# Pooled attention and two feed-forward networks on one core: the probability transpose as one vector instruction and twenty copies inside SBUF

## The chip, the core and the metric

The kernel runs on one core of a Trainium2 chip. The core has a matrix engine (TensorE, PE in the profile, with its weight loads shown as PEld), a vector engine (VectorE, DVE), a scalar engine (ScalarE, ACT), a general engine (GpSimd, POOL) and an engine that here only issues transfers (SyncE, SP). SBUF is the on-chip memory, with 128 partitions; PSUM is the memory that TensorE writes. The metric is the device time of one execution in microseconds (us). The kernel before took 1600.52 us (median of 3 runs, 1599.71 to 1601.85).

## The reference

```python
# q, k, v: (8 batches, 8 heads, 576 tokens, 64), float32
k_p = k.reshape(B, H, 72, 8, D).mean(axis=3)         # pooled over 8 tokens
v_p = v.reshape(B, H, 72, 8, D).mean(axis=3)
scores = (1 / sqrt(D)) * q @ k_p.T                   # 576 x 72 per head
attn = exp(scores - max); attn = attn / (sum(attn) + 1e-9)
x = (attn @ v_p) as 4608 tokens x 512
a, b = x @ w1, x @ w2                                # 512 -> 1024
x2 = (a * b) @ w3 @ w_out                            # 1024 -> 1024 -> 512
h = x2 @ w_in2                                       # 512 -> 2048
out = (h * sigmoid(1.702 * h)) @ w_out2              # 2048 -> 512
```

The weights arrive as float64 and are converted on the chip.

## The kernel before, in words

Every large product is made of three float32r passes: an operand is held as a rounded "hi" part and the exact rest "lo", and hi*hi, hi*lo and lo*hi are added in PSUM (`mm3`, L95 to L97). A TensorE instruction multiplies 128 rows by 512 columns.

The work has three stretches. First w3 @ w_out is formed, while the weights are converted (`Conv`) and the first batch's attention runs beside it. Then comes the first network: nine blocks of 512 tokens, and in each block eight steps f. A step makes a and b for 128 of the 1024 features (24 matmuls into the PSUM tiles wk0 and wk1, one tile for a and one for b), forms u = a * b (ACT copies a out of PSUM on L517, DVE multiplies on L518, ACT and POOL split it on L90 and L91), and two steps later adds u's contribution to x2 (12 matmuls into the four tiles acc). At the end of a block x2 is copied out (L486, L488) and stored to DRAM by SP (L489). Last comes the second network, of the same form.

Attention is done in 32 groups, a pair of heads of one batch each. A group is cut into pieces, and the function `tick` emits one piece at a time between the matmuls: two ticks in each step f, four ticks to a group. The pieces, for group n:

- `g0`: k and q are turned on DVE (L229 into the tile kT, L230 into qT), k is summed over the pool (L232, tile ks), and SP issues the loads of the next group's k and q (8 loads, L203).
- `g1`: scores on TensorE into wk2 and wk3 (L246, ten matmuls), maximum and difference on DVE (L251, L253) into the tile s_t, tokens on partitions.
- `g2`: the exponential on ACT (L261). `g_va` beside it averages v on POOL (L291 to L299) and loads the next v (L223, L224).
- `g3`: sum, reciprocal and normalisation on DVE (L267 to L270). Then the probabilities must be turned so that keys lie on partitions: p0 holds 128 keys, p1 the remaining 16, padded to 32. For the first four groups TensorE does that in `g4` (L318 to L329). For the 28 others DVE does it with 32x32 block transposes: 20 instructions (L281), one for each of 5 key blocks and 4 token blocks, which write the turned blocks to their final place. This is the part that changes.
- `g4`: p0 and p1 are split into ph and pt (ACT L335, L337, L338; POOL L336, L339).
- `g6`: probabilities times values on TensorE (L347 to L350, four matmuls for each of two halves, into wk2 and wk3), and the result is split into the block's input x (ACT L357, DVE L358).

A block of the first network needs, of all four head pairs, the tokens that it covers, so block b waits for group 4b+3. The tiles kT, s_t, p0, p1, ph, pt and qT have one buffer each: who writes one waits for the last reader of its previous content. wk2 and wk3 serve both the scores and the products with the values.

The order in which the instructions stand on each engine isn't the order of the code: a list scheduler reorders them when the program is built, by the code's order as priority and by its own estimate of when each instruction becomes ready. On the chip each engine then works through its own list strictly in order. SP too: a transfer that waits holds up those behind it. Transfers on SP signal eight semaphores in turn, so the ninth waits until the first has landed.

Of the kernel before, what the change touches and what calls it, by code (L numbers as in the profile page):

```python
# [7 lines left out]
F32 = mybir.dt.float32  # L8
# [9 lines left out]
P = 128  # L18
# [4 lines left out]
def pooled_attention_moe_moe2(  # L23
# [10 lines left out]
    w_out2: bass.AP,  # L34
    out: bass.AP,
):
    """Matrix products in three float32r passes: every operand x is held as
    hi = x rounded to 12 significant bits and lo = x - hi (exact), and
    x*y = hi*hi + hi*lo + lo*hi.  The scores take plain float32 products.
    Features lie on partitions and tokens along the free axis up to the last  # L40
    product, which puts tokens back on partitions."""
    nc = tc.nc
    B, H, S, D = q.shape
    NT, DM = out.shape
# [4 lines left out]
    w1, w2, w3, w_out, w_in2, w_out2 = (w.bitcast(U32) for w in (w1, w2, w3, w_out, w_in2, w_out2))  # L49
# [8 lines left out]
    TT = (S + P - 1) // P  # L58
    KW = 2 * SK
    PW = 160  # L60
# [9 lines left out]
    free = [(slot_p, i) for i in range(NSLOT)]  # L70
    held = {}
# [10 lines left out]
    def give(*ts):  # L82
        for t in ts:
            free.append(held.pop(id(t))[1:])
# [6 lines left out]
        lo_eng.tensor_tensor(out=dst[:, 1], in0=src, in1=f32(dst[:, 0]), op=ALU.subtract)  # L91

    def mm3(o, a, a_sl, b, b_sl, first, last):
        """o += a[:, a_sl].T @ b[:, b_sl] of two hi/lo pairs."""
        nc.tensor.matmul(o, a[:, 0, a_sl], b[:, 0, b_sl], start=first, stop=False)  # L95
        nc.tensor.matmul(o, a[:, 0, a_sl], b[:, 1, b_sl], start=False, stop=False)  # L96
        nc.tensor.matmul(o, a[:, 1, a_sl], b[:, 0, b_sl], start=False, stop=last)  # L97
# [7 lines left out]
    def sl(i, n=P):  # L105
        return slice(i * n, (i + 1) * n)

    class Conv:
        """float64 words (low, high) to float32, rounded to nearest, then to hi/lo.
        |w| < 2^-119 stays below that bound, but not exact."""  # L110

        def __init__(self):
            self.todo, self.staged, self.line = [], [], [None, None]
# [19 lines left out]
                self.staged.append((t, turn, done))  # L133

        def step(self):
            """float32 of the next chunk, transpose of the last, hi/lo of the one before."""
            new = None
            if self.staged:
                t, turn, done = self.staged.pop(0)
                lo_w, hi_w = t[:, :, 0], t[:, :, 1]  # L140
                w = cv_p[0].tile([P, T], F32, name="cv", tag="cv", bufs=4)
                wu = w.bitcast(U32)
                nc.scalar.activation(w, hi_w.bitcast(F32), AF.Copy, scale=2.0 ** -112)  # L143
                nc.scalar.activation(lo_w.bitcast(I32), lo_w, AF.Copy, scale=2.0 ** -29)
                nc.vector.tensor_scalar(  # L145
                    out=wu, in0=wu, scalar1=4, scalar2=1,
                    op0=ALU.logical_shift_left, op1=ALU.logical_shift_right)
                nc.vector.scalar_tensor_tensor(  # L148
                    out=wu, in0=hi_w, scalar=0x80000000, in1=wu,
                    op0=ALU.bitwise_and, op1=ALU.bitwise_or)  # L150
                nc.gpsimd.tensor_tensor(  # L151
                    out=w.bitcast(I32), in0=w.bitcast(I32), in1=lo_w.bitcast(I32), op=ALU.add)
                give(t)
                new = [w, turn, done]
            mid, old = self.line
            if mid and mid[1]:
                mid[0] = mid[1](mid[0])
            key = old[2](old[0]) if old else None
            self.line = [new, mid]
            self.load()  # L160
            return key
# [7 lines left out]
    with tc.tile_pool(name="pa", bufs=1) as pa:  # L169
        cv_p[0] = pa  # L170

# [1 line left out]
        mask = pa.tile([P, 2, D], F32, name="mask")  # L173
        nc.gpsimd.memset(mask, 1.0 / POOL)
        nc.gpsimd.affine_select(
            out=mask[:, 0], in_=mask[:, 0], compare_op=ALU.is_gt, fill=0.0,
            base=SK, pattern=[[0, D]], channel_multiplier=-1)
        nc.gpsimd.affine_select(
            out=mask[:, 1], in_=mask[:, 1], compare_op=ALU.is_ge, fill=0.0,
# [5 lines left out]
        s_t = pa.tile([P, TT, PW], F32, name="s_t")  # L185
# [6 lines left out]
            out=ident, in_=ident, compare_op=ALU.is_equal, fill=0.0,  # L192
# [2 lines left out]
        vt = pa.tile([96, 2 * D], F32R, name="vt")  # L195
        nc.gpsimd.memset(f32(vt), 0.0)

# [1 line left out]
        g_q, g_k, g_v, g_s = {}, {}, {}, {}  # L199

        def load_blocks(dst, src, b, hp):
# [61 lines left out]
        def g3(n):  # L263
            r = g_s.pop(n)
            pv = s_t[:, :, :KW].rearrange("p t (a s) -> p t a s", s=SK)
            rv = r.rearrange("p (t a) -> p t a", a=2)
            nc.vector.tensor_reduce(out=rv, in_=pv, op=ALU.add, axis=AX.X)  # L267
            nc.vector.tensor_scalar_add(r, r, 1e-9)
            nc.vector.reciprocal(out=r, in_=r)
            nc.vector.tensor_tensor(  # L270
                out=pv, in0=pv, in1=rv.unsqueeze(3).to_broadcast([P, TT, 2, SK]), op=ALU.mult)
            p0 = pa.tile([P, TT, P], F32, name="p0", tag="p0")
            p1 = pa.tile([32, TT, P], F32, name="p1", tag="p1")
            g_s[n] = (p0, p1)
            if n < NPE:
                return
            for r in range(5):
                for c in range(4):
                    nt = TT if 32 * (c + 1) <= S - (TT - 1) * P else TT - 1
                    dst = p0[32 * r:32 * r + 32] if r < 4 else p1[:32]  # L280
                    nc.vector.transpose(  # L281
                        out=dst[:, :nt, 32 * c:32 * c + 32],
                        in_=s_t[32 * c:32 * c + 32, :nt, 32 * r:32 * r + 32])

        def g_va(n):
            # values, averaged over the pool, in blocks of two heads
            vr, tr = g_v.pop(n), vtr
            a = pa.tile([P, 4 * D], F32, name="va", tag="va")
            at = pa.tile([32, 4 * D], F32, name="vat", tag="vat")
            for d, s in ((a, vr), (at, tr)):  # L290
                nc.gpsimd.tensor_tensor(out=d, in0=s[:, :4 * D], in1=s[:, 4 * D:], op=ALU.add)  # L291
                nc.gpsimd.tensor_tensor(
                    out=d[:, :2 * D], in0=d[:, :2 * D], in1=d[:, 2 * D:], op=ALU.add)
                nc.gpsimd.tensor_tensor(out=d[:, :D], in0=d[:, :D], in1=d[:, D:2 * D], op=ALU.add)
            vf = pa.tile([P, 2, D], F32, name="vf", tag="vf")
            nc.gpsimd.tensor_tensor(
                out=vf, in0=a[:, :D].unsqueeze(1).to_broadcast([P, 2, D]), in1=mask, op=ALU.mult)
            vtf = pa.tile([32, D], F32, name="vtf", tag="vtf")
            nc.gpsimd.tensor_scalar_mul(vtf, at[:, :D], 1.0 / POOL)  # L299
            g_v[n] = (vf.rearrange("p a d -> p (a d)"), vtf)  # L300
            v_load(n + 1)
# [93 lines left out]

        wo_s, wp_s, w1_s, w2_s, b_s1, b_s2 = {}, {}, {}, {}, {}, {}

# [1 line left out]
        NIT = DF1 // P  # L399
        w3_s = {}  # L400

# [13 lines left out]
            return done  # L415

        def w3_mm(key):
            """The products that the chunk that came last makes possible."""
            if isinstance(key, int):
                jts, its = [key], [it for it, jh in seen if jh == key // 4]  # L420
                seen_o.append(key)
            else:
                its, jts = [key[0]], [j for j in seen_o if j // 4 == key[1]]
                seen.append(key)
            for it in its:
                for j in jts:
                    n = n_mm[it] = n_mm.get(it, 0) + 1
                    mm3(acc[it % 4], w3_s[it, j // 4], sl(j % 4), wo_s[j], slice(0, T),
                        n == 1, n == NIT)
                    n4 = n_mm[it, j // 4] = n_mm.get((it, j // 4), 0) + 1  # L430
                    if n4 == 4:
                        give(w3_s.pop((it, j // 4)))
                        seen.remove((it, j // 4))
                    if n == NIT:
                        w = wp_s[it] = take()
                        split(w, acc[it % 4], nc.vector)

        n_mm, seen, seen_o = {}, [], []
        for half in range(2):
            for jh in range(2):  # L440
                for i in range(4):
# [4 lines left out]
                    it = half * 4 + i  # L446
# [20 lines left out]
        while tick_n[0] < 20:  # L467
            tick()

# [1 line left out]
        u_s = {}  # L471
        pend = []

# [28 lines left out]
        for blk in range(NB):  # L502
            x = [x_slot(blk, c) for c in range(KM)]
            for f in range(NF1):
# [11 lines left out]
                a = pa.tile([P, T], F32, name="a", tag="a", bufs=2)  # L516
                nc.scalar.copy(a, pa_)  # L517
                nc.vector.tensor_tensor(out=a, in0=pb_, in1=a, op=ALU.mult)  # L518
                u = u_s[blk, f] = take()
# [27 lines left out]
            conv.staged = st  # L547
        conv.todo = rest

# [1 line left out]
    with tc.tile_pool(name="pb", bufs=1, reuse_waits="tile") as pb_p:  # L551
        for i in range(5):
            free.append((pb_p, NSLOT + i))
# [21 lines left out]
        for blk in range(NB):  # L575
            x = x2n[blk]
            for f in range(NF2):
# [5 lines left out]
                a = pb_p.tile([P, T], F32, name="sg", tag="sg", bufs=3)  # L583
                nc.scalar.activation(a, ps, AF.Sigmoid, scale=1.702)  # L584
                nc.vector.tensor_tensor(out=a, in0=ps, in1=a, op=ALU.mult)  # L585
                g = g_sl[blk, f] = take()
# [45 lines left out]
```

## Time and profile before

| | |
|---|---|
| median of 3 timed runs | 1600.52 us (1599.71 to 1601.85) |
| profiled execution, first to last instruction (span) | 1599.4 us; the page gives no other time for it |
| PE busy | 1536.5 us, 96% |
| DVE busy | 756.8 us, 47% |
| ACT busy | 587.2 us, 37% |
| POOL busy | 714.2 us, 45% |
| granted TensorE clock, mean over the span | 0.982 of full speed |
| transfers on SP's queue | 195392 packets, 94.40 MB, 22.4% of 16 DMA engines' span |

A busy share is an average over the whole span. The first network's stretch runs from about 140 to 800 us; attention of the 28 groups whose transpose changes is over by about 655 us. In the profile a row "idle before <- X" names what ended the wait. Matmuls overlap, so a matmul's own duration (0.39 us) is longer than the distance to the next one.

### The profile page before, as it was taken

The numbers are of one execution on the slowest core, as the hardware profiler recorded it, in microseconds if no ns is written. First come the engines' busy times: TensorE is split into PE (matmuls) and PEld (weight loads), VectorE is DVE, ScalarE is ACT, GpSimd is POOL, SyncE is SP. The second block draws the span as 40 slices with busy tenths as digits, with TensorE's granted clock in tenths as the row PEclk, the third lists the DMA queues.
The fourth block names the chain that finished last, engine by engine and source line by source line (L and its number), as shares of the span: only waits on it lengthen the run. The fifth ranks groups of instructions, "written<-read, shape, count | busy, mean of one in ns | idle before, by whom it ended". The sixth has DMA issues, their size and how long they took to land.

```text
span 1599.4 us, 19097 instructions
## 1 busy us (share of the span) xinstructions
PE 1536.5 (96%) x6920; PEld 1267.0 (79%) x6920; DVE 756.8 (47%) x1458; ACT 587.2 (37%) x1130; POOL 714.2 (45%) x748
## 2 busy tenths in 40 slices
PE   5867999999999999999998999999999999999998
PEld 3645888888888888888786888888888888888887
DVE  8999987878787877214585111111111111111111
ACT  6874443433343334225554222222222222223221
POOL 6789654455555544225777232323222232323221
PEclk9977999999999999999999999999999999999999
DMA  9973232323232310024430000000010000000000
GB/s 277 244 156 58 52 72 50 78 49 72 52 72 45 75 46 34 27 80 158 146 104 27 27 27 27 20 32 20 9 40 14 33 20 33 21 27 14 27 0 27
DMA packets 195488, 95.62 MB, mean 60 GB/s; under 512 B 155457, under 2 KB 171841, under 8 KB 195393
## 3 DMA queue, kind: packets, MB, share of 16 engines
q1 hardware_dynamic: 195392, 94.40, 22.4%
q8 instruction: 54, 0.88, 0.2%
q14 instruction: 42, 0.34, 0.1%
HBM read 75.50 MB, written 18.87 MB: 59 GB/s over the span
## 4 chain that ended last, share of the span: by engine, by line
PE 82%; DVE 8%; issue 3%; DMA 2%; ACT 2%; POOL 2%; SPq 1%; DVEq 0%; POOLq 0%; ACTq 0%
PE wk L95 15%; PE wk L96 15%; PE wk L97 15%; PE acc L97 11%; PE acc L96 11%; PE acc L95 11%; DVE cv L148 2%; PE wk L246 2%; DVE cv L145 2%; DVE s L91 2%; DMA s<-in_moe_w_out_dram 1%; DVE p L281 1%; DMA s<-in_moe_w_dram 1%; POOL s L91 1%; ACT s L90 1%
## 5 line engine op out<-in xcount | busy, mean ns | idle before, releaser
L95 PE MATMUL wk<-s,s 128*128 128x512 f32 x1152 | 453.5, 395 | 7.6 <-DVE a L518 4.3
L96 PE MATMUL wk<-s,s 128*128 128x512 f32 x1152 | 451.4, 392 | 2.0 <-DVE s L358 2.0
L97 PE MATMUL wk<-s,s 128*128 128x512 f32 x1152 | 450.8, 392 | 1.4 <-DVE s L91 1.4
L91 POOL TENSOR_TENSOR s<-sg,s 128x512 fp32r<-128x512 f32 x144 | 188.6, 1310 | 508.8 <-ACT s L90 508.8
L585 DVE TENSOR_TENSOR sg<-wk,sg 128x512 f32<-128x512 f32 x144 | 99.6, 692 | 619.5 <-ACT sg L584 619.5
L97 PE MATMUL acc<-s,s 128*128 128x512 f32 x928 | 363.7, 394 | 9.5 <-DVE s L91 5.1
L95 PE MATMUL acc<-s,s 128*128 128x512 f32 x928 | 364.7, 395 | 4.3 <-ACT s L90 4.3
L96 PE MATMUL acc<-s,s 128*128 128x512 f32 x928 | 364.4, 393 | 1.6 <-DVE s L91 1.1
L95 PEld LDWEIGHTS wk<-s,s 128*128 128x128 f32 x1152 | 217.7, 189 | 54.5 <-DVE a L518 5.6
L97 PEld LDWEIGHTS wk<-s,s 128*128 128x128 f32 x1152 | 217.9, 189 | 47.5 <-DVE s L91 1.8
L96 PEld LDWEIGHTS wk<-s,s 128*128 128x128 f32 x1152 | 217.8, 189 | 46.9 <-DVE s L358 2.4
L584 ACT ACTIVATE sg<-wk 128x512 f32<-128x512 f32 x144 | 86.1, 598 | 410.9 <-PE wk L97 410.8
L97 PEld LDWEIGHTS acc<-s,s 128*128 128x128 f32 x928 | 175.6, 189 | 48.6 <-DVE s L91 8.2
L95 PEld LDWEIGHTS acc<-s,s 128*128 128x128 f32 x928 | 175.4, 189 | 41.5 <-ACT s L90 7.2
L96 PEld LDWEIGHTS acc<-s,s 128*128 128x128 f32 x928 | 175.8, 189 | 38.1 <-POOL s L91 1.8
L91 POOL TENSOR_TENSOR s<-a,s 128x512 fp32r<-128x512 f32 x72 | 94.1, 1307 | 215.8 <-ACT s L90 174.9
L281 DVE STREAM_TRANSPOSE p<-s_t 32x160 f32<-32x160 f32 (+1 forms) x560 | 178.4, 319 | 10.8
L151 POOL TENSOR_TENSOR cv<-cv,s 128x512 int32<-128x512 int32 x72 | 105.4, 1465 | 71.9 <-DVE cv L148 52.1
L90 ACT CAST s<-sg 128x512 fp32r<-128x512 f32 x144 | 89.4, 621 | 112.0 <-DVE sg L585 111.0
L518 DVE TENSOR_TENSOR a<-wk,a 128x512 f32<-128x512 f32 x72 | 49.5, 687 | 78.1 <-PE wk L97 66.4
L148 DVE SCALAR_TENSOR_TENSOR cv<-s,cv 128x512 uint32<-128x512 uint32 x72 | 80.5, 1127 | 1.0
L145 DVE TENSOR_SCALAR cv<-cv 128x512 uint32<-128x512 uint32 x72 | 61.2, 857 | 30.9 <-ACT cv L143 30.7
(91 smaller groups left out, 1360.6 us busy)
## 6 DMA issues: line engine op xcount, KB each, us to landing
s<-in_moe_w_dram SPq DMA_DIRECT2D x32, 512.0 KB, 6.8
s<-in_moe_w_out_dram SPq DMA_DIRECT2D x24, 512.0 KB, 4.6
kr<-in_k_dram SPq DMA_DIRECT2D x128, 72.0 KB, 2.4
qr<-in_q_dram SPq DMA_DIRECT2D x128, 72.0 KB, 2.5
x2d<-x2o SPq DMA_DIRECT2D x36, 256.0 KB, 2.5
x2r<-x2d SPq DMA_DIRECT2D x36, 256.0 KB, 2.9
out_dram<-o SPq DMA_DIRECT2D x36, 256.0 KB, 2.0
vr<-in_v_dram SPq DMA_DIRECT2D x32, 256.0 KB, 2.7
```

The lines of the kernel that those rows point to most:

```text
L90: nc.scalar.copy(dst[:, 0], src)
L91: lo_eng.tensor_tensor(out=dst[:, 1], in0=src, in1=f32(dst[:, 0]), op=ALU.subtract)
L95: nc.tensor.matmul(o, a[:, 0, a_sl], b[:, 0, b_sl], start=first, stop=False)
L96: nc.tensor.matmul(o, a[:, 0, a_sl], b[:, 1, b_sl], start=False, stop=False)
L97: nc.tensor.matmul(o, a[:, 1, a_sl], b[:, 0, b_sl], start=False, stop=last)
L145: nc.vector.tensor_scalar(out=wu, in0=wu, scalar1=4, scalar2=1, op0=ALU.logical_shift_left, op1=ALU.logical_shift_right)
L148: nc.vector.scalar_tensor_tensor(out=wu, in0=hi_w, scalar=0x80000000, in1=wu, op0=ALU.bitwise_and, op1=ALU.bitwise_or)
L151: nc.gpsimd.tensor_tensor(out=w.bitcast(I32), in0=w.bitcast(I32), in1=lo_w.bitcast(I32), op=ALU.add)
L281: nc.vector.transpose(out=dst[:, :nt, 32 * c:32 * c + 32], in_=s_t[32 * c:32 * c + 32, :nt, 32 * r:32 * r + 32])
L518: nc.vector.tensor_tensor(out=a, in0=pb_, in1=a, op=ALU.mult)
L584: nc.scalar.activation(a, ps, AF.Sigmoid, scale=1.702)
L585: nc.vector.tensor_tensor(out=a, in0=ps, in1=a, op=ALU.mult)
```

## The change

For the 28 groups the 20 DVE instructions of `g3` are replaced by one DVE instruction that turns all 32x32 blocks of s_t in place (128 partitions by 800 columns) into a new tile blk_t. In it every block is turned but still lies on the 32 partitions of its tokens. 20 transfers on SP then copy the blocks from SBUF to SBUF to their rows of p0 (16 transfers) and p1 (4). Each moves 32 partitions by 4 or 5 pieces of 32 numbers (128 bytes), 16 to 20 KB. blk_t shares its one buffer with kT (`tag="kT"`), which grows from 576 to 800 columns. ACT and POOL (`g4`) read p0 and p1 as before.

```diff
-            for r in range(5):
-                for c in range(4):
-                    nt = TT if 32 * (c + 1) <= S - (TT - 1) * P else TT - 1
-                    dst = p0[32 * r:32 * r + 32] if r < 4 else p1[:32]
-                    nc.vector.transpose(
-                        out=dst[:, :nt, 32 * c:32 * c + 32],
-                        in_=s_t[32 * c:32 * c + 32, :nt, 32 * r:32 * r + 32])
+            blk_t = pa.tile([P, TT, PW], F32, name="blk_t", tag="kT")
+            nc.vector.transpose(
+                out=blk_t.rearrange("p t c -> p (t c)"), in_=s_t.rearrange("p t c -> p (t c)"))
+            for c in range(4):
+                nt = TT if 32 * (c + 1) <= S - (TT - 1) * P else TT - 1
+                src = blk_t[32 * c:32 * c + 32, :nt]
+                for r in range(4):
+                    nc.sync.dma_start(
+                        p0[32 * r:32 * r + 32, :nt, 32 * c:32 * c + 32],
+                        src[:, :, 32 * r:32 * r + 32])
+                nc.sync.dma_start(p1[:, :nt, 32 * c:32 * c + 32], src[:, :, P:])
```

The rest of the diff drops comments and docstrings. Lines below L291 move down by 5 in the changed file: L347 to L350 become L352 to L355, L357 and L358 become L362 and L363, L489 becomes L494; the new transpose is L279, its transfers are L285 (to p0) and L288 (to p1).

The scheduler places the work differently. On TensorE, at the start of block 4 (wk0 and wk1 are the tiles of a and b, acc0 to acc3 those of x2; s2_3370 is the part of the block's input that comes from group 19, whose products with the values end on L350; s25_3010 comes from group 17), the rows before are:

```order
L350 MATMUL wk3_70<-pt_4032,vt_99 128x288
L96 MATMUL acc1_64<-s31_3907,s34_1103 128x512
L97 MATMUL acc1_64<-s31_3907,s34_1103 128x512
...
L97 MATMUL wk0_67<-s30_3190,s38_1138 128x512
L95 MATMUL wk1_68<-s1_2818,s6_1164 128x512
L96 MATMUL wk1_68<-s1_2818,s6_1164 128x512
L95 MATMUL wk0_67<-s2_3370,s38_1138 128x512
L97 MATMUL wk1_68<-s1_2818,s6_1164 128x512
L95 MATMUL wk1_68<-s25_3010,s6_1164 128x512
L96 MATMUL wk1_68<-s25_3010,s6_1164 128x512
L96 MATMUL wk0_67<-s2_3370,s38_1138 128x512
```

Group 19's products end 19 matmuls ahead of the first one that needs their result; the step's remaining wk matmuls, 12 acc matmuls and the scores of the next group follow. In the changed program, where the same input part is called s2_3394, the place reads:

```order
L353 MATMUL wk3_70<-ph_4063,vm_98 128x288
L354 MATMUL wk3_70<-ph_4063,vm_98 128x288
L355 MATMUL wk2_69<-pt_4064,vt_99 128x288
L355 MATMUL wk3_70<-pt_4064,vt_99 128x288
L95 MATMUL wk0_67<-s2_3394,s38_1140 128x512
L95 MATMUL wk1_68<-s2_3394,s6_1166 128x512
L96 MATMUL wk0_67<-s2_3394,s38_1140 128x512
L97 MATMUL wk0_67<-s2_3394,s38_1140 128x512
L96 MATMUL wk1_68<-s2_3394,s6_1166 128x512
L97 MATMUL wk1_68<-s2_3394,s6_1166 128x512
L246 MATMUL wk3_70<-kbd_89,qT_87 128x144 x2
L246 MATMUL wk2_69<-kbd_89,qT_87 128x144 x3
```

Group 19's products (L352 to L355) have moved down behind 18 of the step's 24 wk matmuls and behind all acc matmuls that are due, and the first matmul that needs their result follows L355 directly. Blocks 5, 6 and 7 begin in the same way. In blocks 1, 2 and 3 the order is similar, but 5, 1 and 4 acc matmuls stand between L355 and the first wk matmul that needs the result, and the ten scores of the next group are put between the step's last wk matmuls.

On SP, at the end of block 0 (kr, qr and vr, vtr are the loads of k, q and v, x2d the stores of x2), the rows before are:

```order
L203 DMA kr<-in_k_dram 32x18x32 x4
L203 DMA qr<-in_q_dram 32x18x32 x4
L489 DMA x2d_71<-x2o 128x512 x3
L223 DMA vr<-in_v_dram 128x512
L224 DMA vtr<-in_v_dram 16x512
L489 DMA x2d_71<-x2o 128x512
```

In the changed program, from the end of one group's copies to the start of the next group's:

```order
L288 DMA p_1967<-blk_t 32x4x32
L223 DMA vr<-in_v_dram 128x512
L224 DMA vtr<-in_v_dram 16x512
L203 DMA qr<-in_q_dram 32x18x32 x3
L494 DMA x2d_71<-x2o 128x512 x4
L285 DMA p_2160<-blk_t 32x5x32 x4
L288 DMA p_2161<-blk_t 32x5x32
```

All four x2 stores of the block now stand ahead of the next group's 20 copies, which are issued back to back, four to p0 and one to p1 in turn.

## Rows read from the trace of the kernel before

**Rows 1.** The page: busy time by engine, and the chain that ended last.

```profile
PE 1536.5 (96%) x6920; PEld 1267.0 (79%) x6920; DVE 756.8 (47%) x1458; ACT 587.2 (37%) x1130; POOL 714.2 (45%) x748
...
PE 82%; DVE 8%; issue 3%; DMA 2%; ACT 2%; POOL 2%; SPq 1%; DVEq 0%; POOLq 0%; ACTq 0%
```

**Rows 2.** Windows: length, busy by engine (instructions), PEclk, DMA share, GB/s.

```profile
120.00:145.00 25.00, 14.61 (x47) 9.86 (x48) 24.25 (x46) 11.36 (x29) 22.65 (x26) 0.64 0.28 55
145.00:200.00 55.00, 55.00 (x258) 46.11 (x256) 50.68 (x117) 24.57 (x55) 41.55 (x59) 0.97 0.28 55
200.00:600.00 400.00, 399.44 (x1925) 337.72 (x1924) 320.75 (x779) 156.98 (x352) 207.55 (x297) 1.00 0.28 61
```

**Rows 3.** What PE waited for, 200 to 660 us: total, times, longest.

```profile
PE wk L246 <- DVE s L358: 0.6, 1, 0.6
```

**Rows 4.** Groups by line and shape, 200 to 600 us: busy us, mean ns, idle before.

```profile
L281 DVE STREAM_TRANSPOSE p<-s_t 32x160 f32<-32x160 f32 x210 | 70.2, 334 | 5.1
L281 DVE STREAM_TRANSPOSE p<-s_t 32x128 f32<-32x128 f32 x210 | 63.6, 303 | 3.4
...
L229 DVE STREAM_TRANSPOSE kT<-kr 128x576 f32<-128x576 f32 x21 | 16.1, 765 | 0.0
...
L517 ACT COPY a<-wk 128x512 f32<-128x512 f32 x43 | 25.2, 586 | 52.1 <-PE wk L97 51.8
```

**Rows 5.** Timeline of one group and the next, by engine: start, length (us).

```profile
319.89 0.90 DVE L270 TENSOR_TENSOR s_t<-s_t,nm 128x720 f32<-128x720 f32 x1
...
333.98 0.73 DVE L232 TENSOR_REDUCE ks<-kT 128x72 f32<-128x576 f32 x1
...
338.57 0.90 DVE L270 TENSOR_TENSOR s_t<-s_t,nm 128x720 f32<-128x720 f32 x1
339.57 0.99 DVE L281 STREAM_TRANSPOSE p<-s_t 32x160 f32<-32x160 f32 x3
...
335.84 0.81 ACT L261 ACTIVATE s_t<-s_t 128x720 f32<-128x720 f32 x1
...
329.56 1.43 POOL L339 TENSOR_TENSOR pt<-p,pt 32x576 fp32r<-32x576 f32 x1
...
330.98 1.39 PE L246 MATMUL wk<-kbd,qT 128*128 128x144 f32 x10
...
338.37 0.29 PE L347 MATMUL wk<-ph,vm 128*128 128x288 f32 x1
```

**Rows 6.** Timeline of PE, neighbouring matmuls; and ACT and DVE reading what PE wrote.

```profile
317.88 0.39 PE L96 MATMUL wk<-s,s 128*128 128x512 f32 x1
318.10 0.39 PE L97 MATMUL wk<-s,s 128*128 128x512 f32 x1
...
320.09 0.30 PE L350 MATMUL wk<-pt,vt 96*128 96x288 f32 x1
...
320.53 0.39 ACT L357 CAST s<-wk 128x288 fp32r<-128x288 f32 x1
...
400.48 0.42 DVE L358 TENSOR_TENSOR s<-wk,s 128x256 fp32r<-128x256 f32 x1
```

**Rows 7.** Timeline of SP: start and length of transfer issues (us).

```profile
5.78 7.65 SPq L203 DMA_DIRECT2D kr<-in_k_dram  x4
...
221.49 1.93 SPq L203 DMA_DIRECT2D kr<-in_k_dram  x4
223.69 1.93 SPq L203 DMA_DIRECT2D qr<-in_q_dram  x4
...
231.74 0.38 SPq L223 DMA_DIRECT2D vr<-in_v_dram  x1
```

**Rows 8.** Windows again: 1 us in which k and q loads land.

```profile
223.40:224.40 1.00, 1.00 (x6) 0.84 (x5) 0.26 (x1) 0.98 (x2) 0.00 (x0) 1.00 0.85 137
```

**Rows 9.** The page, DMA issues: count, KB each, median us to landing.

```profile
kr<-in_k_dram SPq DMA_DIRECT2D x128, 72.0 KB, 2.4
```

**Rows 10.** Timeline of PE where the first network begins.

```profile
144.50 0.80 PE L95 MATMUL wk<-s,s 128*128 128x512 f32 x1 [0.75 <-ACT a L517]
```

## The prediction

> **What bounds the kernel now.** I read the page's busy table and chain first: TensorE is busy 96% of the span and carries 82% of the chain that ended last; DVE, which the change relieves, is busy 47% and carries 8% [rows 1]. A chain is a mean over stretches, so next come windows. From 145 to 200 us TensorE is busy 55.00 of 55.00 us, from 200 to 600 us 399.44 of 400, at a granted clock of 1.00 [rows 2]; its list of waits for 200 to 660 us has one entry, 0.6 us [rows 3]. Inside the attention stretch there is therefore nothing for DVE to give back: TensorE always has work at its full clock (2.4 GHz). Only 120 to 145 us differs: TensorE is busy 14.61 of 25 us at a clock of 0.64, while DVE is busy 24.25 us [rows 2], and the first network's start still waits 0.75 us [rows 10].
>
> **What goes.** In 400 us, 210 + 210 transposes cost 70.2 + 63.6 us at 334 and 303 ns [rows 4]. A group has ten of each: 10 x 0.334 + 10 x 0.303 = 6.4 us, and 28 groups 178 us of DVE. By rows 2 and 3 almost all of it lies beside a full TensorE: its worth on the path is at most the waits named above.
>
> **What comes on DVE.** One transpose of 128 x 800. The nearest row is the same operation over 128 x 576, 765 ns [rows 4]. No less than that, and by columns no more than 765 x 800 / 576 = 1.06 us; I take 1.0, 28 us in all. DVE is 150 us better off.
>
> **What comes on SP: 20 transfers per group.** No row shows a transfer inside SBUF, so both its issue and its landing are bounded. The issues of k and q (576 pieces of 128 bytes each, against 128 to 160 here) stand (223.69 - 221.49) / 4 = 0.55 us apart, that of v 0.38 us long [rows 7]. The far end is the first burst of loads, 7.65 / 4 = 1.9 us each [rows 7]. I take 0.45, between the near rows, since the pieces are fewer than those of k. A k load lands 2.4 us after its issue [rows 9]; with two 72 KB loads to a microsecond the 16 engines are 85% busy [rows 8], so a copy of 16 to 20 KB is about 0.15 us of their time, and 20 are 3 us, less than their issue. A copy that lands at once is the lower end, and a landing longer by some microseconds the upper. A burst takes 19 x 0.45 + 2.4 = 11 us where the twenty transposes took 6.4.
>
> **Is the burst hidden?** A group's period is 338.57 - 319.89 = 18.68 us [rows 5]. From the start of a group's scores (330.98) the transposes begin 339.57 - 330.98 = 8.6 us later [rows 5]. With 1.0 us of transpose, about 0.3 of handing over and the burst, the probabilities lie at 8.6 + 1.0 + 0.3 + 11 = 20.9 us, that is 2.2 us after the next group's scores have begun. ACT takes them up no earlier anyway: it is held for the next exponential until 335.84 + 0.81 - 330.98 = 5.7 us after those scores [rows 5]; then the splits of p0 and p1 run to about 9.4 us (ACT 0.7 us each, POOL's 1.43 [rows 5]). In the changed order TensorE arrives at the products after 42 matmuls: matmuls stand 0.2267 us apart [rows 6], 9.5 us, and the scores themselves take about 1.2, so 10.7 us. The copies fit with some 3.5 us to spare before ACT is late, an issue pitch of 0.45 + 3.5 / 19 = 0.63. The second loop is the shared buffer: the next group's k can be turned only when all 20 copies have read blk_t. Transpose 1.0, issues 20 x 0.45 = 9, landing 2.4, k's transpose 0.77 and pooling 0.73, scaling 0.9 [rows 4, 5], and small handoffs give 14.9 of the 18.68 us; it binds from a pitch of 0.64. On SP the copies (9.0) share the queue with eight loads (8 x 0.55) and two of v (0.9): 14.3 us of 18.68. At each block's end four stores of x2 stand ahead of a burst and wait for the last evictions, about 5.8 us; there the spare is 1.3 us, used up from a pitch of 0.52. So at 0.45 all is hidden, but not by much. The Trainium skill (DMA: Bandwidth & Descriptors, Rules for kernel authors) speaks against this change: many small transfers should be one large one, since under 64 KB one pays mostly overhead. Row and rule agree that most of a 72 KB load's 2.4 us is not transfer; what they differ on is whether 20 overheads overlap, and that is weighed below.
>
> **What the new order costs.** This is the term I trust most, for it stands in the order and not in unknown prices. Before, a group's products end 19 matmuls (4.3 us) ahead of the first matmul of a block that needs their result. Now that matmul follows directly in blocks 4 to 7, and one acc matmul (block 2) or four or five (blocks 3 and 1) lie between. TensorE works in order, so it must stand through the eviction: the last product starts at 320.09 and runs 0.30, ACT begins 0.14 later, at 320.53, and takes 0.39 for 288 columns; DVE follows with 0.42 for the lo part [rows 6]. In block 4 only the first half (256 columns) is needed, whose product ends one matmul (0.13) earlier: 0.30 + 0.14 + 0.37 + 0.06 - 0.26 = 0.61 us of stall, and 0.13 more for the lo part behind two matmuls: 0.74. Blocks 5 to 7 need fewer columns: about 0.65, 0.58, 0.50. Together 2.5 us. Block 2 needs both halves: 0.75. In blocks 1 and 3 acc matmuls hide it, leaving 0.1 each for scores put between waiting matmuls, and block 2 another 0.1. In block 7 no scores follow, so ACT's copy of a, 0.586 us [rows 4], lies open: 0.5. In block 6 only 27 matmuls (6.1 us, 7.3 with the scores) stand between group 28's scores and group 27's products, which are ready at about 9.4 us if ACT keeps its order: 0 to 2.1, I take 1.1. Sum 2.5 + 0.75 + 0.3 + 0.5 + 1.1 = 5.15 us, from 2.5 (if evictions overlap more than I see) to 8.
>
> **What the start gives.** DVE's relief can shorten the wait of 0.75 [rows 10] and little else, since TensorE's order is the same there up to the first network: I take -0.5, between 0 and the stretch's whole idle time, 25 - 14.61 = 10.4 us [rows 2].
>
> **Sum.** 1599.4 + 5.15 - 0.5 = 1604.05 us of span. The median of the timed runs, 1600.52, lies 1.1 us above the profiled span (no other time is given for that execution); added, 1605.2 us, 0.3% slower.
>
> **Rivals.**
> - *The copies become the bound.* Place: SP's queue and the buffer that blk_t shares with kT. Price: each 0.1 us of pitch adds 2.0 us to the loop of 28 groups. It decides from 0.52 at the seven block starts and from 0.64 everywhere. At 0.70 the loop is 0.06 x 20 = 1.2 us too long in some 22 groups: about +26, 1631 us; at 1.9, 25 us too long: +690. For it: the 1.9 us row and 560 new transfers. Against: that row is a queue filled at the program's start, and the other issues stand at 0.55 or less. The skill's rule taken at its strictest, each landing's 2.4 us paid in turn, makes a burst 48 us, 37 more than above; less the 3.8 spare, 28 x 33 = +930, 2535 us. The rows speak against it: four k loads are issued in 2.2 us, under one landing time. I give that 0.02 of the 0.21 for this rival.
> - *Faster.* Place: 120 to 145 us, where DVE is busy 24.25 of 25 us and TensorE idles 10.4. If DVE is what holds that stretch, three groups' transposes gone and the toll at the low end: up to 8 us off and 2.5 on, 1595 us. Against it: the first groups still turn on TensorE, and most of the change lies behind 145 us. It decides if the first network starts over 5 us earlier. 0.09.
> - *No difference.* The order's toll is mostly hidden (evictions overlap what I count as serial, ACT reaches group 27 in time): 2.5 less a start gain of 1 to 2, about 1601.5. 0.21.
>
> **How the numbers follow.** The forecast (copies hidden, toll paid at the block starts) has 0.49 for itself, own range 1602.5 to 1609. About 0.2%, 3.2 us, is what a measurement of this kernel can tell from no change. Slower by more: 0.46 of the forecast's 0.49 and 0.20 of the copies' 0.21: 0.66. Faster by more: 0.08 of its 0.09. The rest, 0.26, is within 0.2%. The range, 1598 to 1632, leaves out the faster case and the copies' dear half.
>
> **What would show it.** Right: DVE's busy time falls from 757 to about 605 us; L279 shows x28 at about 1.0 us; L285 and L288 issues stand about 0.45 us apart; TensorE's new waits are L95 and L96 for ACT L362 and DVE L363, 0.4 to 0.8 each, in blocks 2 and 4 to 7, and one on L352 or L355 near block 6. Wrong: waits on L246 or L352 in every group (the copies bind), a first network that starts microseconds earlier, or no waits at the block starts.

## The result and the profile after

The changed kernel takes 1617.08 us (median of 4 runs, 1616.88 to 1617.84) against 1600.12 us before on the same chip: ratio 1.0103, 95% interval [1.0088, 1.0117], some 17 us slower. Its profiled execution has a span of 1615.5 us, 16.1 us more than before's.

The page of the changed kernel, busy time by engine and the chain that ended last (compare [rows 1]):

```profile
PE 1546.7 (96%) x6920; PEld 1267.4 (78%) x6920; DVE 620.3 (38%) x926; ACT 586.0 (36%) x1130; POOL 721.7 (45%) x748
...
PE 58%; SPq 15%; POOL 7%; DVE 7%; DMA 5%; issue 5%; ACT 2%; DVEq 0%; POOLq 0%; ACTq 0%
```

DVE lost 136 us of work, and the kernel became slower all the same. SP's queue, 1% of the chain before, now carries 15%. The timeline of SP for one group's copies and the loads behind them shows why:

```profile
333.40 2.53 SPq L285 DMA_DIRECT2D p<-blk_t  x4
336.04 0.59 SPq L288 DMA_DIRECT2D p<-blk_t  x1
336.67 2.54 SPq L285 DMA_DIRECT2D p<-blk_t  x4
339.26 0.60 SPq L288 DMA_DIRECT2D p<-blk_t  x1
339.90 2.53 SPq L285 DMA_DIRECT2D p<-blk_t  x4
342.48 0.60 SPq L288 DMA_DIRECT2D p<-blk_t  x1
343.12 3.35 SPq L285 DMA_DIRECT2D p<-blk_t  x4
346.51 0.60 SPq L288 DMA_DIRECT2D p<-blk_t  x1
347.21 0.54 SPq L223 DMA_DIRECT2D vr<-in_v_dram  x1
347.85 0.37 SPq L224 DMA_DIRECT2D vtr<-in_v_dram  x1
348.27 2.04 SPq L203 DMA_DIRECT2D kr<-in_k_dram  x4
350.35 2.12 SPq L203 DMA_DIRECT2D qr<-in_q_dram  x4
```

Five copies begin 336.67 - 333.40 = 3.27 us apart, then 3.23: 0.645 us each, and it is the issue itself that lasts (0.60). The next group's copies begin at 352.58, 19.2 us after these, where TensorE's period before was 18.68 [rows 5]. Twenty copies, eight loads and two of v take 20 x 0.645 + 8 x 0.53 + 0.9 = 18.0 us; four x2 stores a block come on top. SP has become as full as TensorE. And it is SP that is late, not what it is to copy: between 200 and 640 us it stood still for blk_t only three times, 1.9 us in all.

```profile
SPq L285 <- DVE blk_t L279: 1.9, 3, 1.0
```

What TensorE waited for from 200 to 660 us (compare [rows 3], 0.6 us in all):

```profile
PE wk L355 <- POOL pt L344: 4.2, 6, 1.3
PE wk L352 <- ACT ph L340: 2.0, 4, 1.1
PE wk L353 <- POOL ph L341: 1.4, 2, 1.0
PE wk L95 <- ACT s L362: 1.0, 4, 0.3
PE wk L246 <- DVE s L363: 0.2, 1, 0.2
```

The first three, 7.6 us, are probabilities that come late; the last two, 1.2 us, are evictions (the copies of a product out of PSUM) that the new order lays open. One of the longest stands where block 4 begins. In the timeline there (PE's products, and who feeds them) ACT starts on ph when the copies have landed, POOL follows with ph and pt, and TensorE stands 1.28 us in front of L355, then for the eviction:

```profile
445.75 0.67 ACT L340 CAST ph<-p 128x576 fp32r<-128x576 f32 x1 [4.75 <-DMA p<-blk_t]
...
446.50 1.43 POOL L341 TENSOR_TENSOR ph<-p,ph 128x576 fp32r<-128x576 f32 x1 [9.14 <-ACT ph L340]
...
448.01 2.00 POOL L344 TENSOR_TENSOR pt<-p,pt 32x576 fp32r<-32x576 f32 x1
...
448.50 0.29 PE L354 MATMUL wk<-ph,vm 128*128 128x288 f32 x1
450.07 0.53 PE L355 MATMUL wk<-pt,vt 96*128 96x288 f32 x2 [1.28 <-POOL pt L344]
450.51 0.67 ACT L362 CAST s<-wk 128x256 fp32r<-128x256 f32 x2 [0.51 <-PE wk L355]
450.93 0.73 PE L95 MATMUL wk<-s,s 128*128 128x512 f32 x2 [0.33 <-ACT s L362]
```

Some 0.6 us of this wait is POOL's own: pt takes 2.00 us here, 1.43 in the median of the 32 groups; why, no run tells. A view of waits understates such a stall, because a matmul's own length hides part of it: from L354 to L355 pass 1.57 us where 0.13 is the pitch, a stall of 1.44 and not 1.28. The matmul behind the stall costs too: the two L355 last 0.53 us together, 0.44 where no stall stands before them.

The windows of the changed kernel (compare [rows 2]) show idle time and one loss that neither wait list has:

```profile
140.00:150.00 10.00, 9.93 (x43) 8.25 (x43) 7.32 (x15) 4.58 (x10) 9.78 (x17) 0.87 0.18 27
200.00:600.00 400.00, 392.50 (x1848) 324.95 (x1847) 202.25 (x352) 146.90 (x332) 207.77 (x293) 0.99 0.40 77
600.00:700.00 100.00, 98.22 (x451) 81.56 (x450) 41.87 (x74) 35.86 (x77) 38.80 (x46) 0.98 0.29 65
...
525.00:530.00 5.00, 2.32 (x9) 1.36 (x8) 3.72 (x5) 3.85 (x9) 4.15 (x5) 0.83 0.71 117
530.00:535.00 5.00, 4.83 (x16) 4.17 (x16) 2.18 (x5) 2.34 (x7) 1.90 (x6) 0.50 0.24 37
610.00:615.00 5.00, 5.00 (x21) 4.39 (x20) 2.67 (x6) 1.82 (x5) 2.56 (x6) 0.66 0.43 90
```

At block 5's start TensorE was busy 2.32 of 5 us, and in the next 5 us its clock stood at 0.50, the lower level of 1.2 GHz. At block 6, behind another stretch of stalls, it fell again. That costs at most 0.17 x 5 + 0.50 x 5 + 0.34 x 5 = 5.05 us on top of the stalls; for about 1 us of it TensorE stood idle anyway, so some 4.5. In the other direction, the first network begins sooner. The same window of the kernel before, and the first product a * b of before (L518) and after (L523):

```profile
140.00:150.00 10.00, 9.25 (x30) 7.20 (x29) 9.64 (x26) 5.43 (x12) 9.69 (x16) 0.57 0.10 30
...
148.31 0.68 DVE L518 TENSOR_TENSOR a<-wk,a 128x512 f32<-128x512 f32 x1
```

```profile
144.83 0.68 DVE L523 TENSOR_TENSOR a<-wk,a 128x512 f32<-128x512 f32 x1
```

It comes 3.5 us earlier: DVE is free sooner, the wait of [rows 10] is gone, and TensorE reaches its full clock several us earlier (0.87 against 0.57 in the window). Also, behind the attention stretch the clock falls three times in the profile of the kernel before (the two windows below, and 0.70 from 860 to 865 us) and once in that of the changed kernel (0.78 from 860 to 865 us). The two falls more cost the kernel before some 0.34 x 5 + 0.33 x 5 = 3.3 us:

```profile
780.00:785.00 5.00, 5.00 (x15) 3.98 (x16) 3.29 (x4) 3.99 (x7) 4.32 (x4) 0.66 0.75 243
845.00:850.00 5.00, 5.00 (x17) 3.95 (x16) 4.26 (x6) 3.00 (x5) 4.83 (x4) 0.67 0.01 3
```

The account of the 16.1 us: idle time from 145 to 700 us, 0.61 + 7.50 + 1.78 = 9.9 against 0.6 before, is +9.3; the clock there +4.5; what the waits hide, about 0.16 on each of 24 stalls, +4, and 0.1 on the matmul behind most of them, about +2.5; the start -3.5; the two falls that before has more, -3.3. That is 13.5; some 2.6 us are left unassigned.

### The profile page after: what moved, and what is told of

It is laid out like the page before. It is cut to its first block, busy times and chain, and to the rows that moved or that the text cites. A ratio compares the mean times of both kernels' runs of the same rounds, so it can differ in the third digit from the quotient of the medians.

```text
span 1615.5 us, 19393 instructions
## 1 busy us (share of the span) xinstructions
PE 1546.7 (96%) x6920; PEld 1267.4 (78%) x6920; DVE 620.3 (38%) x926; ACT 586.0 (36%) x1130; POOL 721.7 (45%) x748
## 4 chain that ended last, share of the span: by engine, by line
PE 58%; SPq 15%; POOL 7%; DVE 7%; DMA 5%; issue 5%; ACT 2%; DVEq 0%; POOLq 0%; ACTq 0%
SPq L285 11%; PE wk L95 10%; PE wk L97 10%; PE wk L96 10%; PE acc L97 9%; PE acc L96 9%; PE acc L95 9%; SPq L288 2%; DVE cv L145 2%; DMA p<-blk_t 2%; DVE cv L148 2%; POOL pt L344 2%; POOL s L91 1%; DVE s L91 1%; DMA kr<-in_k_dram 1%
## 5 line engine op out<-in xcount | busy, mean ns | idle before, releaser
L341 POOL TENSOR_TENSOR ph<-p,ph 128x576 fp32r<-128x576 f32 x32 | 46.9, 1467 | 161.2 <-ACT ph L340 157.2
L523 DVE TENSOR_TENSOR a<-wk,a 128x512 f32<-128x512 f32 x72 | 49.1, 682 | 96.7 <-PE wk L97 86.0
L90 ACT CAST s<-a 128x512 fp32r<-128x512 f32 x72 | 44.6, 619 | 109.2 <-DVE a L523 108.7
```

The lines of the kernel that those rows point to most:

```text
L90: nc.scalar.copy(dst[:, 0], src)
L341: nc.gpsimd.tensor_tensor(out=ph[:, 1], in0=s0, in1=f32(ph[:, 0]), op=ALU.subtract)
```

## The experiments

Theory "issue": the products (probabilities times values) wait because SP needs 0.645 us for each copy, and 20 fill its queue. Rivals: the landing or the bytes of the copies; the buffer that blk_t shares with kT; the order's toll alone.

**Half of the copies from another queue.**

```diff
+                eng = nc.scalar if c % 2 else nc.sync
...
-                    nc.sync.dma_start(
+                    eng.dma_start(
...
```

> The copies with odd c (10 of 20) are issued from ACT's queue instead of SP's; nothing else is edited. Theory 'issue' (SP's issues, 0.645 us each, 20 x 0.645 + 8 x 0.53 + 0.9 = 18.0 us a group, are what the products wait for): a burst takes half as long, TensorE's waits for ph and pt go, time 1597 to 1602 us. Rival 'landing' (the engines or the landing of the copies bind): the burst is as long as before, 1615 to 1618. Rival 'ACT pays': ten issues of 0.6 us hold ACT's own splits and exponentials up, above 1604.

Measured: 1609.39 us, ratio 1.0050 [1.0034, 1.0066]. TensorE's waits, 140 to 660 us:

```profile
PE wk L95 <- ACT a L523: 4.7, 3, 3.7
PE wk L95 <- DVE a L524: 2.4, 5, 0.6
```

The waits for ph and pt are gone, as "issue" says; products stand early again. The time did not come back, because the rival "ACT pays" holds too: ACT issues ten copies of 0.64 us in its own list, and a is copied late, worst where the first network starts (3.7 us).

**blk_t in a buffer of its own.**

```diff
-            kT = pa.tile([P, S], F32, name="kT", tag="kT")
-            nc.vector.transpose(out=kT, in_=kr.rearrange("p g d -> p (g d)"))
+            kT = kr.rearrange("p g d -> p (g d)")
+            nc.vector.transpose(out=kT, in_=kT)
```

> k is turned in place in its load buffer, so that blk_t has a buffer to itself and the next k need not wait for the 20 copies. Theory 'shared buffer' (the loop copies landed -> kT -> ks -> scores -> blk_t of 19.0 us against TensorE's 18.68 binds): waits for ph and pt go, 1604 to 1608 us (what the order at block starts costs stays). Theory 'issue': SP is still full, 18.0 us of 18.68 and 0.5 for the x2 stores, so it stays at 1611 to 1617 us.

Measured: 1633.01 us, 1.0201 [1.0181, 1.0221]: neither. Giving up the shared buffer did not help. But the scheduler also moved the products still later, and k's loads, now behind a full queue, came late (DVE waits for them 18.9 us, 12 times, 200 to 600 us). The run can't weigh the buffer by itself.

**Loads on ACT's queue.**

```diff
-                nc.sync.dma_start(
+                nc.scalar.dma_start(
                     dst[32 * c:32 * c + 32],
```

(and the two loads of v)

> The loads of k, q and v (10 a group, about 5 us of issue) go from SP's queue to ACT's; the 20 copies stay on SP and blk_t still shares kT's buffer. Theory 'issue' in the sense of a full SP queue: SP has 13 us a group, waits go, 1604 to 1609 us. Theory 'shared buffer': the loop is unchanged, 1613 to 1618 us.

Measured: 1669.44 us, 1.0425 [1.0399, 1.0451]: a miss for both. From 145 to 200 us TensorE is busy only 42.54 of 55 us at a clock of 0.77; ACT, in order, is late with loads, splits and evictions. It speaks of ACT's list, not of SP's.

**Six transfers through DRAM in place of twenty copies.**

```diff
...
+            nc.sync.dma_start(b_d, blk_t)
+            bv = b_d.rearrange("(c i) t k -> i t c k", i=32)
+            for r in range(4):
+                nc.sync.dma_start(
+                    p0[32 * r:32 * r + 32].rearrange("i t (c k) -> i t c k", k=32),
+                    bv[:, :, :, 32 * r:32 * r + 32])
+            nc.sync.dma_start(p1.rearrange("i t (c k) -> i t c k", k=32), bv[:, :, :, P:])
```

> blk_t is stored to DRAM in one transfer and read back into place in five (four to p0, one to p1): 6 issues a group instead of 20, but two landings in turn and pieces of 128 bytes from DRAM. Theory 'issue': 6 x 0.6 + 2 x 2.5 = 9 us against 15 for the burst, waits go, 1596 to 1602 us. Rival 'landing': two landings and 2900 small pieces a group are no faster than the copies, 1612 us or more.

Measured: 1600.14 us, 0.9996 [0.9986, 1.0005]. More bytes and two landings in turn (2.4 and 3.0 us), but few issues: from 200 to 600 us the stretch is as full as before,

```profile
200.00:600.00 400.00, 400.00 (x1932) 338.89 (x1931) 211.18 (x377) 154.08 (x354) 208.46 (x297) 1.00 0.49 106
```

and the loss is gone. TensorE's order went back too: 27 matmuls stand between a group's scores and its products, as before, where the changed kernel has 27 to 73. The start's gain is spent on one early wait of 3.1 us, from 187 us on.

**One piece in five.** All 20 copies, each a fifth or a quarter of the size:

```diff
-                nt = TT if 32 * (c + 1) <= S - (TT - 1) * P else TT - 1
+                nt = 1
```

Here, and in the runs with sixteen copies and with none, the later groups also keep the tiles p0 and p1 of the fourth group (not in the diffs shown); what isn't moved keeps old values there.

> All 20 copies of a group stay, but each moves 32 pieces of 128 bytes instead of 128 or 160 (one token block of five; the rest of the probabilities is not moved). Theory 'issue per transfer': issues still 0.60 to 0.65 us apart, waits for ph and pt as in the changed kernel, 1612 to 1618 us. Rival 'issue per piece' or 'landing': issues come closer together or land earlier, waits go, 1602 to 1607 us.

Measured: 1611.78 us, 1.0070 [1.0056, 1.0085], just under the range of "issue". SP's timeline for half a group:

```profile
349.69 2.42 SPq L289 DMA_DIRECT2D p<-blk_t  x4
352.22 0.52 SPq L292 DMA_DIRECT2D p<-blk_t  x1
352.79 2.49 SPq L289 DMA_DIRECT2D p<-blk_t  x4
355.32 0.60 SPq L292 DMA_DIRECT2D p<-blk_t  x1
```

Issues of 4 KB are nearly as long as those of 20 KB, 0.62 to 0.63 us apart, and the landing falls only from 1.9 to 1.7 us. The bytes and pieces are not the main price. Which of these small gains brings the 5 us less isn't shown.

**Twice as many copies of half the size.**

```diff
-                src = blk_t[32 * c:32 * c + 32, :nt]
+                for lo, hi in ((0, 2), (2, nt)):
+                    src = blk_t[32 * c:32 * c + 32, lo:hi]
...
```

> Each copy is cut in two along the tokens: 40 copies a group, the same bytes. Theory 'issue per transfer': still 0.6 to 0.65 us apart, so SP needs 40 x 0.635 + 5.1 = 30.5 us a group and the loop through the shared buffer some 32; 28 groups x 12 to 13.5 us more than TensorE's 18.68: 1930 to 1990 us. Rival 'issue per piece' (half the pieces, half the time): 1612 to 1625 us.

Measured: 1971.13 us, 1.2317 [1.2291, 1.2342], inside the range of "issue", far from "per piece". The first copies of two groups in a row:

```profile
329.73 2.51 SPq L286 DMA_DIRECT2D p<-blk_t  x4
...
360.93 2.51 SPq L286 DMA_DIRECT2D p<-blk_t  x4
```

A period of 31.2 us, with SP issuing all the time. TensorE waits 167.1 us for ph from 145 to 690 us, at a clock of 0.80 from 200 to 600.

**Sixteen copies (those to p1 left out).**

```diff
-                nc.sync.dma_start(p1[:, :nt, 32 * c:32 * c + 32], src[:, :, P:])
```

> The four copies of a group to p1 are left out (16 keys of 144 are not moved), 16 copies stay. SP has 16 x 0.645 + 5.1 = 15.4 us a group, and TensorE's order comes back close to that of before (group 19's products at the same place as before). Theory 'issue' with its order: waits gone and no toll, 1596 to 1601 us. Rival 'the copies cost in proportion' (16/20 of the loss): about 1613 us.

Measured: 1601.65 us, 1.0006 [0.9996, 1.0015]. A fifth fewer copies takes away nearly the whole loss, not a fifth of it, as relief of a full queue would: SP now stands still for blk_t 30.6 us, 16 times, from 200 to 640 us. TensorE's order came back close to that of before as well, so the run shows both effects together. TensorE's only waits from 145 to 690 us are 2.5 us for ph, mostly in the first block.

**The x2 stores off SP**, to POOL's queue and to ACT's:

```diff
-                    nc.sync.dma_start(x2_d[blk][:, m], st)
+                    nc.gpsimd.dma_start(x2_d[blk][:, m], st)
```

> The four x2 stores of each block go from SP's queue to POOL's (4 x 0.5 us of issue per block off SP); the 20 copies stay on SP, and the products with the values stay as late in TensorE's order as in the changed kernel. Theory 'SP is full' (per block 4 x 18.0 + 2.0 = 74.0 us of SP against 4 x 18.68 = 74.7 of TensorE): 2 us of slack per block come back, the waits for ph and pt shrink by half or more, 1603 to 1609 us. Rival 'shared buffer' (the loop blk_t - copies - kT of 19.0 us binds in every group): 1613 to 1618 us.

> The same, with the x2 stores on ACT's queue. Theory 'SP is full': 1603 to 1610 us. Rival 'shared buffer': 1613 to 1618. Rival 'ACT pays': ACT stands behind each store's wait and issue and is late for the splits, above 1612.

Measured: 1612.50 us on POOL's queue, 1.0076 [1.0061, 1.0091]; 1614.98 on ACT's, 1.0086 [1.0069, 1.0104]. On POOL's queue the waits for ph and pt from 200 to 660 us fall from 7.6 to 1.7 us, so the stores in SP's queue were a large part of what made the probabilities late. But the total came down by 4.6 us, not the 8 or more expected; it missed both ranges and lies 0.5 us below that of "shared buffer". Evictions are now waited for longer, and the clock still fell once (0.83 from 445 to 455 us).

```profile
PE wk L96 <- DVE s L363: 1.5, 2, 1.1
PE wk L95 <- ACT s L362: 1.2, 3, 0.5
PE wk L355 <- POOL pt L344: 1.0, 4, 0.3
PE wk L352 <- ACT ph L340: 0.7, 2, 0.4
```

And SP, relieved, stands still for blk_t five times as long as in the changed kernel (200 to 640 us): with the stores gone, the loop through the shared buffer is the next in line.

```profile
SPq L285 <- DVE blk_t L279: 10.0, 11, 4.8
```

On ACT's queue the same waits for evictions are 6.5 us: ACT paid, inside its expected range and the buffer rival's both.

**DVE's relief alone.** All copies left out:

```diff
-            for c in range(4):
-                ...
+            nc.vector.tensor_copy(p0[:, 0, :1], blk_t[:, 0, :1])
+            nc.vector.tensor_copy(p1[:, 0, :1], blk_t[:32, 0, :1])
```

> The one transpose stays, all 560 copies are left out (two copies of one column by DVE stand in their place, so the probabilities are not moved to their rows). What DVE's relief is worth by itself, with the order of the kernel before. Theory 'issue' (the copies' issues cost the time, DVE's relief is worth the start only): 1595 to 1598 us. Rival 'relief worth nothing': 1600 us. Rival 'the transpose or another part costs': above 1603 us.

Measured: 1596.97 us, 0.9979 [0.9970, 0.9987]. TensorE's order is close to that of before here. That is all that 150 us of DVE time are worth: 3 us.

**Only the first group turned in the new way.**

```diff
+            if not (n < NPE + 1):
...                (the 20 transposes of the kernel before)
+                return
             blk_t = pa.tile([P, TT, PW], F32, name="blk_t", tag="kT")
```

> Only the first of the 28 groups (group 4) is turned by the one transpose and the 20 copies; groups 5 to 31 keep the 20 transposes of the kernel before. Theory 'start': the change's gain of about 3.3 us where the first network begins (TensorE at full clock some 6 us earlier, no wait for a) comes from the relief of DVE in that one group, so this kernel gains it and pays nothing in the blocks: 1596 to 1599 us. Rival: the gain comes with other costs in the first block, 1600 us or more.

Measured: 1597.16 us, 0.9981 [0.9973, 0.9990]: faster than both kernels. It has no wait from 200 to 660 us, its first a * b stands at 145.11, and one group turned in the new way buys the whole gain. It is the version to keep.

**The same with DRAM for that one group.**

> As the kernel that turns only group 4 in the new way, but its probabilities pass through DRAM (one store, five loads) instead of 20 copies. Theory 'start': 1596 to 1599 us. Rival: 1600 us or more.

Measured: 1600.68 us, 1.0000 [0.9992, 1.0009]. The gain is gone; TensorE waits 2.1 us in front of scores between 145 and 200 us. What of that is the longer way through DRAM and what the order, no run tells.

## Why the prediction was right and wrong, point by point

- **The range.** 1617 us lies inside the stated range, 1598 to 1632, and outside the forecast's own, 1602.5 to 1609. The range holds it only because it takes in the cheap half of a rival that I gave 0.21.
- **Direction.** Slower, as forecast, for the reason that the attention stretch had nothing for DVE to give back [rows 2, 3]. The run without copies puts DVE's relief at 3 us. But the loss that I forecast was the order's toll; the larger part of what came is copies that are late.
- **Size: the step that failed is "I take 0.45" for the issue of a copy.** It measures 0.645, above both near rows that I had set as its bounds (0.38 and 0.55 [rows 7]); the far row, 1.9, was needed. I assumed that fewer pieces issue faster; the run with a fifth of the pieces shows that the count of pieces hardly matters. The decision points of the rival "the copies become the bound" (0.52 at block starts, 0.63 to 0.64 everywhere) were passed, so the likeliest case was the wrong one and that rival came true. With the measured price its own working gives (0.645 - 0.52) x 19 = 2.4 us at seven block starts, 17 us, and 1605.2 + 17 = 1622 against 1617 measured. That this is near is in part luck: the waits for probabilities are 7.6 us, not 17, and the clock and what the waits hide, which the working leaves out, make up much of the rest. The sign that I named for it, a wait in every group, did not come either.
- **The x2 stores.** The 5.8 us on which the 0.52 rests has no row behind it; SP issues a block's four stores in 1.9 us, straight behind the loads (469.78 to 471.69 us).
- **Hidden at 0.45?** Can't be shown directly; with sixteen copies, 15.4 us of SP a group, TensorE is busy 399.61 of 400 us from 200 to 600 us, which agrees.
- **The order's toll.** Right in place and nearly in size. From the starts of the rows as in the fence above, stalls for evictions are 0.87 us in block 2 (0.75 and 0.1 forecast), 0.60, 0.48, 0.48 and 0.34 in blocks 4 to 7 (0.74, 0.65, 0.58, 0.50), and 0.43 for a in block 7 (0.5). Group 27's products in front of block 6, forecast at 0 to 2.1, waited about 1.5.
- **Not in the sum at all: the clock.** Stalls close together at blocks 5 and 6 were followed by the lower level, which cost some 4.5 us.
- **The start.** -0.5 forecast, about -3 measured (the run without copies and the one with one group). I had priced the wait and not the clock behind it, though the row at 0.64 [rows 2] was there.
- **DVE.** 1010 ns for the transpose against 1.0 forecast. Busy time is 620.3 us and not 605: other DVE rows grew, the normalisation's product (L270) from 961 to 1135 ns.
- **The rule that I set aside** (the Trainium skill, DMA: Bandwidth & Descriptors, Rules for kernel authors: coalesce many small transfers into one large one) was the right warning: six transfers for twenty took the loss away. Landings paid in turn was my strictest reading of it, which the trace contradicts: copies land 1.9 us after issue and are issued 0.645 us apart.
- **Queue or loop?** DVE waits 92.7 us for copies before it may turn k, so the loop through the shared buffer is tight. But if the loop were what binds, SP would stand idle for blk_t in front of each group's first copy, and it does so for only 1.9 us between 200 and 640 us: the queue comes first, the loop close behind.
- **Open.** What the shared buffer alone costs was not separated: the run that gave blk_t a buffer changed the order too. What the toll costs with the late order and no late data was not run either.

## What to carry to other kernels

Work taken off an engine that isn't the bound is worth only the places where that engine is waited for; here 3 us of 150, all in one group. Before replacing instructions by transfers, multiply their number by an issue time and add the queue's other transfers: a queue that comes as close to full as the bounding engine costs time at the next thing added to it, here the x2 stores at each block's end. And a scheduler that believes in late data moves the consumer next to its own dependents, which lays bare an eviction that had been hidden.

## What the runs showed that was not expected

A copy inside SBUF of 32 to 160 pieces takes about 0.60 us to issue, whatever its size from 4 to 20 KB, longer than a load of k or q of 576 pieces from DRAM (0.51 to 0.53), and as long on ACT's queue as on SP's. Whether the source inside SBUF is the reason isn't shown: in the run with six transfers, the load to p1 back from DRAM takes 0.58 us too.
